# One 2 MB group of output weights loaded with a pattern whose outermost dimension counts 8

## The chip, the core and the metric

The kernel runs on one NeuronCore of a Trainium2 chip. The core has a matrix engine (TensorE, in the profile PE for the products and PEld for loading the stationary operand), VectorE (DVE), ScalarE (ACT), GpSimd (POOL) and SyncE (SP), which here does nothing but issue transfers. Sixteen DMA engines carry the data from the chip's memory (HBM) into the on-chip memory, whose first axis is 128 partitions. The metric is the device time of one execution in microseconds (us).

## The reference

One decoding step of a block: a layer norm, grouped-query attention over a cached K and V, a gated feed-forward branch, and a residual. Everything is float32.

```python
xn = layernorm(x)                               # x: [2, 1, 512]
q = (xn @ wq)                                   # 32 heads of 128
k, v = repeat(k_cache, 4), repeat(v_cache, 4)   # caches: [2, 8 kv heads, 32768, 128]
p = softmax(q k^T * 128**-0.5)
s = (p v).reshape(2, 1, 4096) @ wo              # wo: [4096, 512]
h = relu(xn @ w1 + b1) ** 2                     # w1: [512, 1792]
g = silu(h @ w2 + b2)
return x + s * g
```

The two caches are 268 MB each (256 MiB); with the weights the kernel reads 561 MB and writes 4 KB.

## The kernel before

**Streaming.** There are 16 sequences s (8 kv heads x 2 batch rows; hkv, b = divmod(s, 2)). Each is cut into 4 chunks of 8,192 positions, so there are 64 chunks of K and 64 of V, 4 MB each. A chunk is one transfer: 128 partitions, 32 KB for each. K has two buffers (pool "k"), V has two (pool "v"). A list `loads` holds all transfers in a fixed order, and `issue` sends the next ones on SP's queue as long as the pool of the first has a free buffer; `give`, called after the last use of a buffer, frees one and calls `issue` again. So the order on SP is that of the list, and nothing overtakes.

**One chunk.** `scores` (K): VectorE transposes the chunk in 32 x 32 blocks (L258), TensorE multiplies it with the queries (L263). After the fourth chunk `softmax` runs on VectorE and ScalarE; `probs` transposes the probabilities on TensorE. `values` (V) multiplies them with the V chunk four steps later (L319). At the end of a sequence `values` divides by the sum and puts the sequence's four head outputs into columns of `oT` (L331): partition = position in the head, column = head.

**The output projection.** The 4,096 rows of wo are handled in four groups of 1,024 rows (8 heads), `wo0` to `wo3`, 2 MB each. In a group, partition p holds rows 8p to 8p + 7 of it, one piece of 16 KB: so 16 consecutive partitions hold one head. The head outputs must be brought to the same layout. After every second kv head (L332) VectorE forms `om`: for each of the group's 8 heads, the head's column times a 0/1 selector `sele` (which of 16 blocks of 8 positions a position lies in), 128 x 128 numbers (L335). TensorE multiplies it with `selj` (which of 8 places in the block, L338) and ScalarE copies the result into `oW` (L339). `project` then multiplies `oW[:, i, j]` with `wo` (L401), eight steps for each group.

**The end.** The list's last transfers are: V chunk 60, wo0, V chunk 61, wo1, V chunk 62, V chunk 63 in two halves, wo2, and wo3 in four transfers: rows 0 to 5 of each partition's eight (1.5 MB, L122), then rows 6 and 7 in three pieces of columns (L124: 256, 128 and 128 columns). The program ends with the projections of groups 0 to 2, the first part of group 3, and then for each of the three pieces: projection, product with the gate (L414), a small matmul that also adds the residual (L415), a copy (L416). The result goes out at L417.

The instructions of an engine run in the order in which they are written in the program.

## Time and profile before

| | |
|---|---|
| time, median of 3 runs | 1321.92 us (1321.65 to 1323.48) |
| the profiled execution | 1321.55 us, its span 1319.8 us |
| PE / PEld / DVE / ACT / POOL busy | 865.2 / 300.3 / 646.4 / 69.0 / 27.9 us |
| read from HBM | 561.00 MB, 425 GB/s over the span |
| transfers of wo | 3 of 2,048 KB, 1 of 1,536 KB, 1 of 256 KB, 2 of 128 KB |
| instruction transfers (queue q8) | 52 packets, 0.85 MB |

The span runs from the first to the last instruction in the trace; the profiled execution's own time also holds what lies around it. A page of the profile shows the busy time of each engine, the span in 40 slices (33 us each) with the mean busy share of the 16 DMA engines, the DMA queues, the chain of work that ended last, followed back from the end, and the costliest groups of instructions. A group's row reads: line, engine, operation, output <- input, shape and count | busy time, mean ns of one | idle time of the engine just before, and what ended it. The view of stages gives the same busy times and the DMA share for chosen stretches of the span. An instruction's line in the timeline shows its start, its length and, in brackets, the idle time before it with what ended that.

### The profile page before, as it was taken

Reading aid. Unit: us, or ns where it says so; the run is one execution under the profiler, and the core shown is the slowest. Engines: PE = TensorE matmul, PEld = TensorE weight load, DVE = VectorE, ACT = ScalarE, POOL = GpSimd, SP = SyncE. Lnnn points to the kernel's source line nnn. Section 1 sums busy time; section 2 is a strip of 40 time slices with the busy share of each in tenths; the row PEclk is TensorE's granted clock in tenths of the full one; section 3 lists DMA queues with packets and bytes.
Section 4 is the critical chain, followed back from the end, with each engine's and each line's share of the span. In section 5 each row is a group of like instructions: output and inputs, shape, how many; then the busy total and the mean of one; then the engine's idle time right before and its main releaser. Section 6 shows DMA issues by size and latency. Waiting matters only on the chain.

```text
span 1319.8 us, 15186 instructions
## 1 busy us (share of the span) xinstructions
PE 865.2 (66%) x6710; PEld 300.3 (23%) x6710; DVE 646.4 (49%) x699; ACT 69.0 (5%) x109; POOL 27.9 (2%) x141
## 2 busy tenths in 40 slices
PE   4677765765676666675676666576577657667575
PEld 1222221322222122221222122132222212122121
DVE  3765553554555365355445445455445536535510
ACT  0010000101001010000101000010100101010010
POOL 1000000000000000000000000000000000000000
PEclk9988777787877877877877987787888788788778
DMA  9999999999999999999999999999999999999996
GB/s 412 429 429 428 432 432 433 430 429 432 431 431 428 432 433 429 432 432 429 431 430 433 432 431 429 432 428 434 431 429 432 431 431 431 430 429 434 431 404 284
DMA packets 20626, 561.96 MB, mean 426 GB/s; under 512 B 2249, under 2 KB 3021, under 8 KB 3026
## 3 DMA queue, kind: packets, MB, share of 16 engines
q1 hardware_dynamic: 20548, 561.00, 99.0%
q8 instruction: 52, 0.85, 0.3%
q14 instruction: 12, 0.10, 0.0%
q10 hardware_dynamic: 14, 0.01, 0.0%
HBM read 561.00 MB, written 0.00 MB: 425 GB/s over the span
## 4 chain that ended last, share of the span: by engine, by line
DMA 73%; DVE 21%; PE 3%; issue 3%; DVEq 0%; SPq 0%; ACT 0%; ACTq 0%
DMA k<-in_A_k_cache 69%; DVE kt L258 20%; DMA wo<-in_A_wo 2%; DMA v<-in_A_v_cache 1%; PE q_ps L219 1%; PE o_ps L319 1%; DMA xt<-in_A_x 1%; DVEq L258 0%; PE sc L263 0%; PE y_ps L365 0%; PE qT_ps L230 0%; PE a_ps L401 0%; DVE qr L226 0%; PE s_ps L415 0%; PE y_ps L370 0%
## 5 line engine op out<-in xcount | busy, mean ns | idle before, releaser
L258 DVE STREAM_TRANSPOSE kt<-k 128x1024 f32<-128x1024 f32 x512 | 584.4, 1208 | 423.9 <-DMA k<-in_A_k_cache 422.4
L263 PE MATMUL sc<-kt,qz 128*32 128x256 f32 x4096 | 544.5, 459 | 351.5 <-DVE kt L258 338.7
L263 PEld LDWEIGHTS sc<-kt,qz 128*32 128x32 f32 x4096 | 179.7, 127 | 729.7 <-DVE kt L258 602.9
L319 PE MATMUL o_ps<-v,pT 128*16 128x512 f32 x2048 | 261.2, 605 | 13.3 <-DMA v<-in_A_v_cache 13.3
L319 PEld LDWEIGHTS o_ps<-v,pT 128*16 128x16 f32 x2048 | 69.6, 98 | 155.9 <-issue 125.6
L326 ACT COPY o_sb<-o_ps 128x512 f32<-128x512 f32 x16 | 9.4, 585 | 1080.9 <-PE o_ps L319 1080.9
L295 PE MATMUL pT_ps<-ident,p 128*128 128x128 f32 x128 | 30.2, 412 | 46.7 <-ACT p L282 46.7
L331 DVE COPY oT<-oT_ps 128x4 f32<-128x4 f32 x16 | 2.6, 163 | 99.0 <-PE oT_ps L330 99.0
L242 POOL COPY qz<-qT 32x16 f32<-32x16 f32 x128 | 25.1, 200 | 1060.1 <-PE sc L263 1038.8
L270 DVE TENSOR_REDUCE rm<-sc 128x1 f32<-128x1024 f32 x16 | 19.6, 1224 | 32.1 <-PE sc L263 32.1
L295 PEld LDWEIGHTS pT_ps<-ident,p 128*128 128x128 f32 x128 | 23.7, 213 | 50.8 <-ACT p L282 49.7
L282 ACT ACTIVATE p<-sc,nm 128x1024 f32<-128x1024 f32 x16 | 32.9, 2057 | 25.1 <-DVE nm L279 25.0
L330 PE MATMUL oT_ps<-rs,o_sb 128*128 128x4 f32 x128 | 16.9, 255 | 12.0 <-ACT o_sb L326 12.0
L330 PEld LDWEIGHTS oT_ps<-rs,o_sb 128*128 128x128 f32 x128 | 15.5, 191 | 26.7 <-ACT o_sb L326 26.7
L296 ACT COPY pT<-pT_ps 128x512 f32<-128x512 f32 x32 | 18.7, 585 | 25.0 <-PE pT_ps L295 25.0
L286 DVE TENSOR_SCALAR lh<-selh,l 128x4 f32<-128x4 f32 x16 | 3.7, 229 | 32.9 <-ACT p L282 32.8
L302 DVE RECIPROCAL r<-l_ps 128x4 f32<-128x4 f32 x16 | 2.9, 182 | 33.0 <-PE l_ps L300 33.0
L207 PE MATMUL xnT_ps<-ident,xn 128*128 128x128 f32 x4 | 1.1, 428 | 15.6 <-DVE xn L203 15.6
L226 DVE COPY qr<-q_ps 128x512 f32<-128x512 f32 x8 | 5.3, 690 | 10.3 <-PE q_ps L219 9.8
L219 PE MATMUL q_ps<-wq,xnT 128*32 128x512 f32 x64 | 9.7, 774 | 0.8 <-DVE xnT L208 0.8
L401 PE MATMUL a_ps<-wo,oW 128*32 128x512 f32 (+2 forms) x72 | 9.0, 548 | 1.4 <-DMA wo<-in_A_wo 1.4
L300 PE MATMUL l_ps<-lh,ones 128*128 128x4 f32 x32 | 9.1, 355 | 0.0
(72 smaller groups left out, 98.2 us busy)
## 6 DMA issues: line engine op xcount, KB each, us to landing
k<-in_A_k_cache SPq DMA_DIRECT2D x64, 4096.0 KB, 29.6
v<-in_A_v_cache SPq DMA_DIRECT2D x63, 4096.0 KB, 33.9
wq<-in_A_wq SPq DMA_DIRECT2D x2, 4096.0 KB, 16.7
w<-in_B_w SPq DMA_DIRECT2D x2, 3584.0 KB, 27.7
wo<-in_A_wo SPq DMA_DIRECT2D x3, 2048.0 KB, 26.2
v<-in_A_v_cache SPq DMA_DIRECT2D x2, 2048.0 KB, 18.7
wo<-in_A_wo SPq DMA_DIRECT2D x1, 1536.0 KB
wo<-in_A_wo SPq DMA_DIRECT2D x1, 256.0 KB, 26.6
```

The source lines that it names most:

```text
L219: nc.tensor.matmul(q_ps[32 * g:32 * g + 32, f, :], xnT[:, d, 0:32], wqt[:, d2, cc * 512:(cc + 1) * 512], start=(d == 0), stop=(d == ND - 1))
L242: nc.gpsimd.tensor_copy(t[:, c, :, lo:lo + REP], qT[32 * a:32 * a + 32, b, hkv].rearrange("p h e -> p e h"))
L258: nc.vector.transpose(r.rearrange("p e o w -> p o e w"), kt[:, lo:lo + NO, :].rearrange("p o (e w) -> p o e w", e=4))
L263: nc.tensor.matmul(sc[s][32 * g:32 * g + 32, t // 2, c0:c0 + 256], qz[s % 2][:, c, e, :], kts[g][:, e].rearrange("p o w -> p (o w)"), star ...
L270: nc.vector.tensor_reduce(rm, sc[s], axis=AX.XY, op=ALU.max)
L282: nc.scalar.activation(p.rearrange("p o w t -> p o t w"), sc.pop(s).rearrange("p b (t o w) -> p o (b t) w", t=2, w=32), AF.Exp, bias=nm, s ...
L295: nc.tensor.transpose(t_ps[:, j * P:(j + 1) * P], p[:, 4 * i + j].rearrange("p w t -> p (w t)"), ident)
L296: nc.scalar.copy(sb[:, :, 4 * i:4 * i + 4, :].rearrange("p r o h -> p o r h"), t_ps.rearrange("p (o r h) -> p o r h", o=4, h=REP))
L300: nc.tensor.matmul(t_ps[:, :REP], ones, lh, start=True, stop=True)
L319: nc.tensor.matmul(o[32 * g:32 * g + 16, :], pT[s][:, r0, 4 * i:4 * i + 4, :].rearrange("p o h -> p (o h)"), vt[:, lo:lo + 4, :].rearrange ...
L326: nc.scalar.copy(o_sb, o)
L330: nc.tensor.matmul(t_ps[:, :REP], o_sb[:, i * DH:(i + 1) * DH], r4[:, i, :], start=(i == 0), stop=(i == 3))
```

## The change

Group 2 (`WHALF`) is loaded with another pattern; all other groups stay as they were. Its 1,024 rows are written as (n y j): 16 blocks n of 64 rows, in each 8 blocks y of 8 rows j. The source is walked with y outermost (count 8, 16 KB apart), then n (count 16, 128 KB apart), then 16 KB in one piece; the destination is walked as before, partition by partition. So partition 16 y + n now holds rows 64 n + 8 y to 64 n + 8 y + 7 of the group. Head h of the group (rows 128 h to 128 h + 127) has n = 2 h and 2 h + 1, that is partitions 16 y + 2 h + z with z = 0, 1.

`om` for group 2 (kv head 5, sequences 10 and 11) is therefore written in the order (y, h, z) in place of (h, e). The tile of `om` is now declared as 128 x 128 for all groups and viewed in either order; the other six executions do the same as before. The matmul with `selj`, the copy to `oW` and `project` are unchanged.

```diff
+WHALF = 2
...
     def load_wo(i):
...
         src = wo[i * WG * P:(i + 1) * WG * P, :].rearrange("(p j) e -> p j e", p=P)
-        if i < NWG - 1:
+        if i == WHALF:
+            nc.sync.dma_start(t.rearrange("p j e -> p (j e)"),
+                              wo[i * WG * P:(i + 1) * WG * P, :].rearrange("(n y j) e -> y n (j e)", y=8, j=WG))
+        elif i < NWG - 1:
             nc.sync.dma_start(t, src)
...
-                m = work.tile([P, WG, P // WG], F32, tag="om", name=f"om{s}")
-                nc.vector.tensor_mul(m, oT[:, i * WG:(i + 1) * WG, b:b + 1].to_broadcast([P, WG, P // WG]),
-                                     sele[:, None, :].to_broadcast([P, WG, P // WG]))
+                m = work.tile([P, P], F32, tag="om", name=f"om{s}")
+                oh = oT[:, i * WG:(i + 1) * WG, b]
+                if i == WHALF:
+                    nc.vector.tensor_mul(m.rearrange("p (y h z) -> p y h z", y=8, z=2),
+                                         oh[:, None, :, None].to_broadcast([P, 8, WG, 2]),
+                                         sele.rearrange("p (z y) -> p y z", y=8)[:, :, None, :].to_broadcast([P, 8, WG, 2]))
+                else:
+                    nc.vector.tensor_mul(m.rearrange("p (h e) -> p h e", h=WG),
+                                         oh[:, :, None].to_broadcast([P, WG, P // WG]),
+                                         sele[:, None, :].to_broadcast([P, WG, P // WG]))
                 t_ps = misc(f"oW_ps{s}")
-                nc.tensor.matmul(t_ps[:, :WG], m.rearrange("p h e -> p (h e)"), selj, start=True, stop=True)
+                nc.tensor.matmul(t_ps[:, :WG], m, selj, start=True, stop=True)
                 nc.scalar.copy(oW[:, i, :, b], t_ps[:, :WG])
```

## The prediction

> **What bounds the kernel now.** I read the page first: the busy line, the slices, the DMA queues, the chain.

> ```profile
> span 1319.8 us, 15186 instructions
> PE 865.2 (66%) x6710; PEld 300.3 (23%) x6710; DVE 646.4 (49%) x699; ACT 69.0 (5%) x109; POOL 27.9 (2%) x141
> ...
> DMA  9999999999999999999999999999999999999996
> GB/s 412 429 429 428 432 432 433 430 429 432 431 431 428 432 433 429 432 432 429 431 430 433 432 431 429 432 428 434 431 429 432 431 431 431 430 429 434 431 404 284
> ...
> q1 hardware_dynamic: 20548, 561.00, 99.0%
> q8 instruction: 52, 0.85, 0.3%
> ...
> DMA 73%; DVE 21%; PE 3%; issue 3%; DVEq 0%; SPq 0%; ACT 0%; ACTq 0%
> ```

> No compute engine is near full; the 16 DMA engines are, in every slice but the last. 430 GB/s over 16 engines is 26.9 GB/s for one. At that pace 16,384 bytes, one partition's row of an output-weight group, take 0.609 us; a 2 MB group spread over 16 engines (eight rows each) takes 4.87 us, and the first part of the last group (1.5 MB, six rows of eight) 3.65 us. The kernel streams 561 MB, so only the amount and its spread over the engines count. The last slice, 284 GB/s, is where they don't all work to the end. Next: the stages of the tail (columns: start and end, length, busy time of PE, PEld, DVE, ACT, POOL, clock, mean DMA share, GB/s).

> ```profile
> 1300.00:1306.00 6.00, 3.75 (x36) 0.64 (x28) 0.00 (x0) 0.49 (x1) 0.00 (x0) 1.00 0.98 413
> 1306.00:1307.00 1.00, 0.85 (x8) 0.85 (x8) 0.00 (x0) 0.10 (x1) 0.00 (x0) 1.00 0.95 347
> 1307.00:1308.00 1.00, 0.33 (x4) 0.27 (x4) 0.46 (x2) 0.00 (x0) 0.00 (x0) 1.00 0.57 239
> ...
> 1310.00:1311.00 1.00, 0.91 (x6) 0.00 (x0) 0.00 (x0) 0.00 (x0) 0.00 (x0) 1.00 0.51 187
> 1311.00:1312.00 1.00, 0.00 (x0) 0.00 (x0) 0.00 (x0) 0.00 (x0) 0.00 (x0) 1.00 0.26 96
> 1312.00:1313.00 1.00, 0.74 (x8) 0.44 (x12) 0.00 (x0) 0.00 (x0) 0.00 (x0) 1.00 0.27 82
> 1313.00:1314.00 1.00, 1.00 (x12) 0.15 (x4) 0.00 (x0) 0.00 (x0) 0.00 (x0) 1.00 0.01 4
> ```

> The share falls in steps: eight engines are done at about 1306.9, four at 1311.0, four at 1313.1. So one half runs ahead of the other by 4.1 to 6.2 us. Where the lag may come from is in the queue rows above: 0.85 MB of instruction transfers, if they fall on eight engines only, are 106 KB each, 3.9 us at 26.9 GB/s. Last, the chain and the timeline of the end.

> ```profile
> 1285.71 26.42 DMA wo<-in_A_wo
> 1312.12 0.14 issue
> 1312.26 1.96 PE a_ps L401 x12
> ...
> 1317.37 0.28 DVE fin L416
> ```

> ```profile
> 1303.48 1.91 PE L319 MATMUL o_ps<-v,pT 128*16 128x512 f32 x16 [1.63 <-DMA v<-in_A_v_cache]
> ...
> 1308.28 0.17 ACT L339 COPY oW<-oW_ps 128x8 f32<-128x8 f32 x1 [2.18 <-PE oW_ps L338]
> ...
> 1308.84 2.07 PE L401 MATMUL a_ps<-wo,oW 128*32 128x512 f32 x13
> ...
> 1312.26 1.91 PE L401 MATMUL a_ps<-wo,oW 128*32 128x512 f32 x16 [1.35 <-DMA wo<-in_A_wo]
> ```

> Two things set the end. The last piece of v (1303.48) leads through its products and group 2's projection to 1308.84 + 2.07 = 1310.91, where PE is free. The first part of group 3 lands at 1312.12, and PE starts it 1.35 us late. From there to the span's end are 1319.8 - 1312.12 = 7.7 us, which nothing here changes; the last three pieces of group 3 land under that work.

> **The change part by part.** Group 2 (the loop's i == 2) is the last full transfer before group 3. Its source becomes 8 blocks x 16 rows x 16 KB. What is moved stays 128 rows, 2 MB, at the same place of SP's queue and with the same wait; the first part and the three pieces of group 3 stay behind it. SP issues as many instructions as before.

> ```profile
> L120 SPq DMA_DIRECT2D wo<-in_A_wo x3: 383/433/1076, 1240.7 to 1285.2; - x3
> ...
> L335 DVE TENSOR_TENSOR om<-oT,sele x8: 291/292/293, 321.6 to 1307.4; 128x128 f32<-128x128 f32 x8
> ...
> L226 DVE COPY qr<-q_ps 128x512 f32<-128x512 f32 x8 | 5.3, 690 | 10.3 <-PE q_ps L219 9.8
> ...
> L258 DVE STREAM_TRANSPOSE kt<-k 128x1024 f32<-128x1024 f32 x512 | 584.4, 1208 | 423.9 <-DMA k<-in_A_k_cache 422.4
> ```

> - Issue on SP: 0.4 to 1.1 us for such a transfer now. The new form might cost from 0.4 less to 1.1 us more. Behind it on SP are only group 3's four issues, and the piece of v ahead of it lands 18 us later (1303.48); taken as 0. Without that cover, 1.1 us.
> - The product with the selector (om): two of its eight executions get another order of reading. The copy with a repeated operand moves 512 elements in 0.69 us, so 128 in 0.17; twice the present 0.29 is the other end. Both executions belong to kv head 5 (sequences 10 and 11 of 16), long before the end, where VectorE waits 422 us in all for K. Taken as 0; uncovered, from -0.2 to +0.6 us. The matmul and copy behind it keep their shapes.
> - The spread over the engines. An outermost count of 8 lets the work be dealt out eightfold: eight engines carry 16 rows of group 2, 16 x 0.609 = 9.74 us, and eight carry none.

> [...] No run here shows a large transfer with such a count.

> Which half is that? No view names engines. [...]

> Now the sum. The half ahead ends at 1306.9, less 4.87 for group 3, 4.87 for group 2 and about 0.2 for small pieces: it begins group 2 at 1297.0. The price that no row shows is that of two engines writing into the same part of the on-chip memory. Now each engine has its own eight rows in every 128-row transfer; with 16 consecutive rows for each of eight engines that ends. The bounds: no sharing, each keeps 26.9 GB/s; or sharing in pairs, each gets half. The nearest rows are the windows: 413 GB/s at a share of 0.98 and 239 at 0.57 are both 26.2 to 26.3 GB/s for one busy engine, so the pace belongs to each path and not to the memory that is read. They don't say at which end of the path the limit sits. I take sharing in pairs: a path that never shows more than 27 GB/s is more easily halved than doubled.

> [...]

> Shared in pairs, group 2 takes 2 x 9.74 = 19.5 us, to 1316.5; the first part of group 3 ends 3.65 later, at 1320.15, 8.0 us after 1312.12. Half of group 2's rows are those that the other eight engines serve, and they are still at work there. While a third engine takes turns, the pairs' four rows each (8 x 0.609 = 4.87 us) take 7.3, to 1304.3: +2.4. On the next four rows the engines met have 1311.0 - 4.87 - 1304.3 = 1.8 or 1313.1 - 4.87 - 1304.3 = 3.9 us of work left, which adds 1.8 to 2.4. After that they are done. So 8.0 + 2.4 + 1.9 = 12.3 us later. PE waits for it, and the 7.7 us behind it stay. The profiled execution took 1321.55 (its span of 1319.8 and 1.75 around it), 0.4 under the median of 1321.92: **1321.55 + 12.3 = 1333.9 us.**

> **The rivals.**

> - No sharing (the other side: not slower). The half ahead ends at 1306.9 + 4.87 = 1311.8, the other at 1313.1 - 4.87 = 1308.2. The first part of group 3 now lands 1.0 before the last end (1313.1 - 1312.1), so at 1310.8; PE is free at 1310.91. PE starts at about 1311.05 in place of 1312.26: 1.2 us won, 1320.7 with the median as base. More than 1.35 can't be had, since the chain through the last v stands behind it: a gain of over 0.2% (2.6 us, about what a measurement can tell from no change) is all but excluded. For it: the imbalance is plain in the windows, and nothing in the trace shows two engines hindering each other. It decides as soon as sharing costs the eight less than 1.3 us of their 9.74.
> - Sharing only with the other half. If each of the eight first writes rows of its own paths and then those of the other eight, it reaches them at 1297.0 + 4.87 = 1301.9, and halves its pace while they work: 4.87 become 9.74, to 1311.6, first part of group 3 at 1315.3: 3.2 us later, 1325. It needs an order of rows that consecutive rows don't give.
> - The eight are those behind. They end at 1313.1 + 4.87: 1326.8 without sharing. [...]
> - The pattern is dealt to 16 engines after all, and nothing changes: 1321.9. For it: still 128 rows of 16 KB on the memory's side.

> **How the numbers follow.** Sharing in pairs 0.45 (its own range 1329.5, which is 1321.55 + 8.0 alone, to 1335.5, with 2.4 twice and 1.1 on SP); no sharing 0.32; sharing with the other half only 0.10; the wrong half 0.07; no effect 0.06. Slower by over 0.2% is 0.45 + 0.10 + 0.07 = 0.62; within it, the two others less 0.02 for a reading that chance puts lower: 0.36; faster 0.02. The range takes in both ends of the unknown price: from 1320.4, a little under the no-sharing case, to 1335.5.

> **What will show it.** In the windows of the tail, a share of about 0.5 from the time the other half is done, at 13 GB/s for a busy engine if paths are shared (share high, GB/s low), at 26 if not. The first part of group 3 lands at about 1324 (forecast) or 1310.8. PE's idle time ahead of group 2's and group 3's projections, now 1.35 us, grows to over 10. With sharing the last pieces of v land later too, by 3 to 5 us after 1303.48; without it they stay. The om rows stay near 0.3 us. The prediction is wrong if the packets of group 2 keep about 0.61 us each.

## The result and the profile after

The changed kernel takes 1336.51 us (median, 1336.40 to 1336.73) against 1321.83 us before on the same chip: a ratio of 1.0107, 95% interval 1.0095 to 1.0119, or 14.7 us more. The direction was forecast, the size was not: 1333.9 was said, with 1335.5 as the upper end. The profiled execution has a span of 1334.6 us (before 1319.8).

The stages of the tail after the change (columns as before: stretch, length, PE, PEld, DVE, ACT, POOL, clock, DMA share, GB/s; a packet counts in the stretch in which it begins, so a share can come out a little over 1):

```profile
1290.00:1296.00 6.00, 2.35 (x12) 0.48 (x16) 0.00 (x0) 0.00 (x0) 0.00 (x0) 0.50 0.99 423
1296.00:1300.00 4.00, 4.00 (x24) 0.67 (x16) 0.00 (x0) 0.00 (x0) 0.00 (x0) 0.57 1.12 279
1300.00:1304.00 4.00, 1.94 (x20) 0.37 (x16) 0.00 (x0) 0.00 (x0) 0.00 (x0) 1.00 0.99 213
1304.00:1308.00 4.00, 0.00 (x0) 0.00 (x0) 0.00 (x0) 0.00 (x0) 0.00 (x0) 0.78 0.95 197
1308.00:1312.00 4.00, 2.25 (x12) 0.49 (x16) 0.00 (x0) 0.00 (x0) 0.00 (x0) 0.50 0.91 199
1312.00:1316.00 4.00, 2.56 (x18) 1.22 (x10) 0.46 (x2) 0.58 (x1) 0.00 (x0) 0.87 0.81 167
1316.00:1320.00 4.00, 1.56 (x4) 0.13 (x3) 0.00 (x0) 0.17 (x1) 0.00 (x0) 0.56 0.54 170
1320.00:1324.00 4.00, 0.66 (x4) 0.20 (x8) 0.00 (x0) 0.00 (x0) 0.00 (x0) 0.50 0.32 116
1324.00:1328.00 4.00, 3.78 (x25) 0.84 (x21) 0.00 (x0) 0.00 (x0) 0.00 (x0) 0.66 0.15 55
```

The kernel before, over the first two of these stretches together:

```profile
1290.00:1300.00 10.00, 6.31 (x36) 1.32 (x40) 0.00 (x0) 0.00 (x0) 0.00 (x0) 0.53 1.02 436
```

Up to 1296 the rate is that of the kernel before. Then the share stays near 1 while the rate falls to half: 213 GB/s at 0.99 is 213 / (16 x 0.99) = 13.4 GB/s for a busy engine, where the kernel before had 26. All 16 engines are busy, and all are slow, not only the eight that carry group 2: in the trace's records of single packets, every 16 KB row that begins between 1297 and 1300 takes 1.16 to 1.27 us, and every 12 KB row (group 3) 0.94 to 0.96, where 0.61 and 0.46 are the rule in the kernel before. After 1316 the share falls in a long tail: few engines are left, and 116 / (16 x 0.32) = 22.7 GB/s says that most of their time they are no longer halved.

The last waits of PE (timeline) and the last chain:

```profile
1309.75 3.54 PE L324 MATMUL o_ps<-v,pT 128*16 128x512 f32 x16 [7.81 <-DMA v<-in_A_v_cache]
...
1323.34 3.58 PE L413 MATMUL a_ps<-wo,oW 128*32 128x512 f32 x16 [5.78 <-DMA wo<-in_A_wo]
...
1327.13 1.91 PE L413 MATMUL a_ps<-wo,oW 128*32 128x512 f32 x16 [0.22 <-DMA wo<-in_A_wo]
```

```profile
1285.06 0.77 SPq L122
...
1285.87 41.12 DMA wo<-in_A_wo
1327.00 0.14 issue
```

The last piece of v is used at 1309.75 in place of 1303.48, group 2 at 1323.34, and the first part of group 3 lands at 1327.00 in place of 1312.12: 14.9 us later. From there to the end are 7.6 us, as before (7.7). What was costed at nothing stayed so: SP's issue took 0.77 us (median of such a transfer before: 0.43) and the reordered product with the selector (L342) as long as the others:

```profile
L346 DVE TENSOR_TENSOR om<-oT,sele x6: 291/292/293, 321.4 to 1315.3; 128x128 f32<-128x128 f32 x6
L342 DVE TENSOR_TENSOR om<-oT,sele x2: 292/293/294, 947.6 to 1025.7; 128x128 f32<-128x128 f32 x2
```

### The profile page after: what moved, and what is told of

The parts are those of the page before. It is cut to its first block, busy times and chain, and to the rows that moved or that the text cites. A ratio compares the mean times of both kernels' runs of the same rounds, so it can differ in the third digit from the quotient of the medians.

```text
span 1334.6 us, 15186 instructions
## 1 busy us (share of the span) xinstructions
PE 867.2 (65%) x6710; PEld 300.4 (23%) x6710; DVE 646.2 (48%) x699; ACT 69.1 (5%) x109; POOL 27.9 (2%) x141
## 3 DMA queue, kind: packets, MB, share of 16 engines
q1 hardware_dynamic: 20540, 561.00, 98.7%
HBM read 561.00 MB, written 0.00 MB: 420 GB/s over the span
## 4 chain that ended last, share of the span: by engine, by line
DMA 73%; DVE 21%; PE 3%; issue 2%; DVEq 0%; SPq 0%; ACTq 0%; ACT 0%
DMA k<-in_A_k_cache 68%; DVE kt L263 20%; DMA wo<-in_A_wo 3%; DMA v<-in_A_v_cache 1%; PE q_ps L224 1%; PE o_ps L324 1%; DMA xt<-in_A_x 1%; DVEq L263 0%; PE sc L268 0%; PE y_ps L377 0%; PE qT_ps L235 0%; PE a_ps L413 0%; DVE qr L231 0%; PE s_ps L427 0%; PE y_ps L382 0%
## 5 line engine op out<-in xcount | busy, mean ns | idle before, releaser
L335 PE MATMUL oT_ps<-rs,o_sb 128*128 128x4 f32 x128 | 16.9, 255 | 12.0 <-ACT o_sb L331 12.0
L335 PEld LDWEIGHTS oT_ps<-rs,o_sb 128*128 128x128 f32 x128 | 15.5, 191 | 27.5 <-ACT o_sb L331 27.5
L231 DVE COPY qr<-q_ps 128x512 f32<-128x512 f32 x8 | 5.3, 690 | 10.3 <-PE q_ps L224 9.8
## 6 DMA issues: line engine op xcount, KB each, us to landing
wo<-in_A_wo SPq DMA_DIRECT2D x3, 2048.0 KB, 26.3
```

The costliest lines, as they stand in the source:

```text
L335: nc.tensor.matmul(t_ps[:, :REP], o_sb[:, i * DH:(i + 1) * DH], r4[:, i, :], start=(i == 0), stop=(i == 3))
```

## The experiments

**The disputed price by itself.** A kernel with loads only, one after the other. Its load functions, without the rest of it:

```diff
+    def plain(n, col):
+        nc.sync.dma_start(t[:n], w[:8 * n, :].rearrange("(p j) e -> p (j e)", j=8))
...
+    def eight(n, col):
+        nc.sync.dma_start(t, w.rearrange("(n y j) e -> y n (j e)", y=8, j=8))
...
+    def near(n, col):
+        nc.sync.dma_start(t, wo[:1088, :].rearrange("(y n j) e -> y n (j e)", y=8, j=8)[:, :16])
...
+    def quarters(n, col):
+        v = w.rearrange("(m r y j) e -> m y r (j e)", m=4, r=4, j=8)
+        for m in range(4):
+            nc.sync.dma_start(t[32 * m:32 * m + 32], v[m])
...
+    def far16(n, col):
+        nc.sync.dma_start(t, w.rearrange("(b a j) e -> a b (j e)", b=8, j=8))
...
+    def split(n, k, col):
...
+        nc.sync.dma_start(t[:n], w[:8 * n, :].rearrange("(q y j) e -> y q (j e)", y=k, j=8))
...
```

`eight` is the changed kernel's pattern, `near` gives each engine 256 KB in one piece of HBM, `far16` has an outermost count of 16.

> This kernel leaves out the whole computation: it only loads parts of wo, one transfer after the other, each after the one before has landed, and writes x's memory out again. Order, each of the first five twice: the group's plain 2 MB load; the changed kernel's pattern (outermost 8, blocks 128 KB apart); outermost 8 with each block of 16 rows contiguous in HBM; the changed kernel's pattern cut into four transfers of 32 partitions (outermost 8, four partitions for each); 16 engines with blocks far apart (256 KB). Then smaller ones: 32 and 64 partitions with outermost 8, 64 with 4, 32 with 2, 8 with 2, 4 with 2. Theory T (engines that write into the same part of the on-chip memory share its path): plain and far apart about 430 GB/s while running, packets of 16 KB in 0.61 us; the pattern and its contiguous variant both about 110 GB/s, packets 1.22 us; four quarters about 215 GB/s, packets 0.61. Of the small ones, 32 with 8 and 32 with 2 run at 0.61, 64 with 8 at 1.22, 8 with 2 at 0.61, 4 with 2 at 1.22. Theory S (the order of reading in HBM): the pattern, the quarters and the far-apart load all slow, the contiguous variant at 0.61. Theory W (eight engines instead of 16, and some of them those that are behind, no sharing): every packet of 16 KB takes 0.61, the patterns with 8 about 215 GB/s.

Stretches from within the transfers (DVE, POOL, clock, DMA share, GB/s). In order: plain; the pattern; contiguous in HBM; quarters; outermost 16; 64 partitions dealt in eights to eight; 64 partitions to four; 32 to two; 8 to two; 4 to two:

```profile
14.50:19.50 5.00, 0.00 (x0) 0.00 (x0) 1.00 0.83 344
24.00:40.00 16.00, 0.00 (x0) 0.00 (x0) 1.00 0.51 111
68.00:84.00 16.00, 0.00 (x0) 0.00 (x0) 1.00 0.51 114
112.00:118.00 6.00, 0.00 (x0) 0.00 (x0) 1.00 0.51 218
136.00:144.00 8.00, 0.00 (x0) 0.00 (x0) 1.00 1.08 227
167.00:173.00 6.00, 0.00 (x0) 0.00 (x0) 1.00 0.47 109
179.00:194.00 15.00, 0.00 (x0) 0.00 (x0) 1.00 0.26 57
200.00:208.00 8.00, 0.00 (x0) 0.00 (x0) 1.00 0.12 53
212.50:214.50 2.00, 0.00 (x0) 0.00 (x0) 1.00 0.11 49
217.20:219.00 1.80, 0.00 (x0) 0.00 (x0) 1.00 0.07 18
```

A share of 0.51 is eight engines. The pattern gives them 111 / (16 x 0.51) = 13.6 GB/s each, and reading in one piece changes nothing (114). The same eight blocks in the same order of reading, but written in fours, run at 26.7 GB/s each (218 at 0.51). So S falls, and W cannot be all: the place of writing decides. Nor is an engine slow by itself when it writes 16 neighbouring partitions: 32 partitions dealt to two engines run at 53 / (16 x 0.12) = 27.6 GB/s each. With 4 partitions for two engines, the four packets took 0.94 to 1.39 us, near the 1.22 that T had said; over their stretch it is 18 / (16 x 0.07) = 16 GB/s for a busy engine. The others fall into two kinds. A busy engine moved 13.6 to 14.5 GB/s with the pattern (111 at 0.51) and with 64 partitions dealt in eights (109 at 0.47) or sixteens (57 at 0.26). It moved 26 to 28 where a transfer held 32 partitions or 8, with at least four for each engine (218 at 0.51, 53 at 0.12, 49 at 0.11). Which partitions share a path, no view shows.

Two things came out otherwise than expected. The load with an outermost count of 16 was said to run at 430 under T; it ran at 227 GB/s with all engines busy. My estimate of the reason, from the half pace of 64 partitions dealt in eights (109 at 0.47): each engine gets eight neighbouring partitions here too and is met there by another; no view shows which engine writes where. Of the two forms here that use all 16 engines, only the plain one, with 128 rows in one dimension on both sides, ran at full pace (344 / (16 x 0.83) = 25.9 GB/s for a busy engine, against 227 / (16 x 1.08) = 13.1). And plain loads of 2 MB that stand alone show 344 over a stretch that holds their ends.

**The same in the kernel.** Group 2 in four transfers of 32 partitions:

```diff
-            nc.sync.dma_start(t.rearrange("p j e -> p (j e)"),
-                              wo[i * WG * P:(i + 1) * WG * P, :].rearrange("(n y j) e -> y n (j e)", y=8, j=WG))
+            parts = wo[i * WG * P:(i + 1) * WG * P, :].rearrange("(q r y j) e -> q y r (j e)", q=4, r=4, j=WG)
+            for q in range(4):
+                nc.sync.dma_start(t[32 * q:32 * q + 32].rearrange("p j e -> p (j e)"), parts[q])
```

(with the selector's product in the matching order, four small instructions for each of the two executions).

> Group 2 as in the changed kernel, the same eight blocks read in the same order by the same count of eight, but as four transfers of 32 partitions, so that each engine writes four neighbouring partitions in each. Theory T: no pairs meet any more; what is left is the meeting with the other eight engines and the doubled work of the eight: 1324 to 1329 us, packets of 0.61 us except where the two halves meet. Theory S: as slow as the changed kernel, 1335 to 1338, packets at 1.2 us. Theory W: as slow as eight engines with double work make it, 1326 to 1328 if two of the eight are behind, and the changed kernel's time is then left unexplained by 9 us.

Measured: 1331.36 us, ratio 1.0074 (1.0059 to 1.0089): 9.8 us lost in place of 14.7. That lies above the 1324 to 1329 of T. Its tail:

```profile
1296.00:1302.00 6.00, 5.44 (x40) 1.05 (x32) 0.00 (x0) 0.00 (x0) 0.00 (x0) 0.79 1.00 428
1302.00:1304.00 2.00, 0.19 (x4) 0.13 (x8) 0.00 (x0) 0.00 (x0) 0.00 (x0) 1.00 1.03 310
1304.00:1310.00 6.00, 4.57 (x28) 1.59 (x20) 0.46 (x2) 0.76 (x2) 0.00 (x0) 0.90 0.88 186
```

Full pace lasts to 1302, which is when the first of the eight (at group 2 since 1297.0) have written their eight rows on partitions 0 to 63 (8 x 0.609 = 4.87 us) and begin on 64 to 127. Then the engines are halved again: 186 / (16 x 0.88) = 13.2 GB/s for a busy one. Beside plain loads (below) the same dealing showed the same two sides: 422 GB/s on partitions 0 to 63, 203 on 64 to 127.

**The place.** `WHALF = 0` in place of 2: the pattern on group 0.

> The pattern on group 0, which is loaded about 45 us before the end with 16 MB still to follow, in place of group 2. If transfers bound the whole stream, the place doesn't matter: the engines lose the same time, 1333 to 1338 us. If only the tail is exposed and the queues ahead take the loss up elsewhere: 1322 to 1326.

Measured: 1344.3 us, ratio 1.0170 (1.0153 to 1.0187), 22.7 us lost; both expectations missed, the first of them in the right direction. Its stages, and its last chain:

```profile
1270.00:1290.00 20.00, 5.56 (x32) 1.03 (x32) 0.00 (x0) 0.00 (x0) 0.00 (x0) 0.67 1.00 224
...
1304.00:1311.00 7.00, 6.92 (x44) 1.34 (x36) 0.00 (x0) 0.00 (x0) 0.00 (x0) 0.68 0.41 150
```

```profile
1259.66 43.00 DMA v<-in_A_v_cache
...
1302.71 6.55 PE o_ps L324 x32
...
1309.28 0.33 SPq L101
...
1309.66 17.40 DMA v<-in_A_v_cache
```

The half pace is there as well, and a second loss comes behind it: from 1304 to 1311 the engines are 59% idle. A chunk of V lands 43.00 us after its issue, PE uses it until 1309.26, and only that frees the buffer for which the next load waits (issued at 1309.28). So here, earlier in the stream, the pattern costs more, not less.

**Who is held up.** Again loads only: a first load and, right behind it without a wait, two plain loads over all 16 engines into other buffers. The first loads:

```diff
...
+    def blocks(lo, n, k):
+        nc.sync.dma_start(t[lo:lo + n], w[:8 * n, :].rearrange("(q y j) e -> y q (j e)", y=k, j=8))
...
+    def low_pairs():
+        blocks(0, 64, 8)
+    def low_apart():
+        blocks(0, 32, 8)
+        blocks(32, 32, 8)
+    def high_apart():
+        blocks(64, 32, 8)
+        blocks(96, 32, 8)
+    def full_pattern():
+        blocks(0, 128, 8)
...
```

> This kernel leaves out the whole computation and only loads. Ten groups of transfers, each group after the one before has landed: a first load into one buffer, and right behind it two plain 1.5 MB loads over all 16 engines (12 KB rows, alone 0.46 us each) into other buffers. The first load is, twice each: plain 2 MB over 16 engines; 64 partitions (0 to 63) dealt to eight engines in eights, so that they meet in pairs; the same 64 partitions dealt in fours, so that they don't meet; partitions 64 to 127 dealt in fours, where each of the eight meets one of the other eight; the changed kernel's full pattern. The question is why all 16 engines ran at half pace in the changed kernel. Theory L (sharing slows only the engines that write into the same part): beside the pairs on 0 to 63 the other eight engines stay at 0.46 us for a 12 KB row, and the core moves about 109 + 217 = 326 GB/s while both run. Theory B (a full path holds up the others too): they slow down as well, to 0.9 us, and the core moves about 220 GB/s. In both: the load dealt in fours on 0 to 63 leaves everybody at full pace (430 GB/s while 16 run), on 64 to 127 every engine is halved (about 217).

Stretches in which the first load and the plain ones run together: plain; in eights on 0 to 63 (both times); in fours on 0 to 63; in fours on 64 to 127; the full pattern:

```profile
22.00:28.00 6.00, 0.15 (x1) 0.00 (x0) 1.00 0.99 423
35.00:40.00 5.00, 0.00 (x0) 0.00 (x0) 1.00 0.99 211
52.00:57.00 5.00, 0.00 (x0) 0.00 (x0) 1.00 1.07 229
80.00:84.00 4.00, 0.00 (x0) 0.00 (x0) 1.00 1.00 422
92.00:97.00 5.00, 0.00 (x0) 0.00 (x0) 1.00 0.99 203
127.00:131.00 4.00, 0.00 (x0) 0.00 (x0) 1.00 1.00 143
```

In fours on 0 to 63 disturbs nobody (422; 377 at a share of 0.94 the other time, 25 GB/s for a busy engine); in fours on 64 to 127 the core falls to 203 (215 the other time). From these two I take it that the other eight engines write to 64 to 127 and are met there only. Yet the load in eights on 0 to 63 brings the whole core to 211 to 229 GB/s. Theory L wanted 326. The trace's records of single packets say the same: between 35 and 40 us no 12 KB row of the plain loads took less than 0.75 us (median 0.95), where 0.46 is the rule from 22 to 28. So the load in eights on 0 to 63 held up all 16 engines: theory B. Where on the way they are held up, no view shows. With the full pattern it is a third, 143 (149 the other time).

**Which eight.** The kernel before, with half of group 2 left out (partitions 64 to 127 are filled with zeros, so the result of that group is not the reference's), the other half dealt in fours to the eight engines of the pattern:

```diff
-        if i < NWG - 1:
+        if i == 2:
+            half = wo[i * WG * P:i * WG * P + 512, :].rearrange("(q r y j) e -> q y r (j e)", q=2, r=4, j=WG)
+            for q in range(2):
+                nc.sync.dma_start(t[32 * q:32 * q + 32].rearrange("p j e -> p (j e)"), half[q])
+            nc.gpsimd.memset(t[64:], 0.0)
+        elif i < NWG - 1:
```

> The kernel before, but of group 2 only 1 MB is loaded, into partitions 0 to 63, dealt in fours to the eight engines of the pattern; the other half of the group is left out (filled with zeros on GpSimd). So the eight have the same eight rows as before and nobody meets anybody; the other eight have 4.87 us less. If the eight of the pattern are those ahead, as the prediction took it: all transfers end by 1308.4, PE starts the last group at about 1311, 1320.3 us. If some of the eight are those behind: a few engines still work to 1311 or 1313, the share of DMA there is their number over 16, and the time stays at 1321 to 1322.

Measured: 1322.01 us, ratio 1.0006 (0.9997 to 1.0016): nothing won with 1 MB less. Its tail:

```profile
1307.00:1308.00 1.00, 0.39 (x3) 0.38 (x4) 0.43 (x2) 0.00 (x0) 0.00 (x0) 1.00 0.28 105
1309.00:1310.00 1.00, 1.00 (x12) 0.34 (x5) 0.00 (x0) 0.00 (x0) 0.00 (x0) 1.00 0.18 69
1310.00:1311.00 1.00, 0.64 (x5) 0.00 (x0) 0.00 (x0) 0.00 (x0) 0.00 (x0) 1.00 0.12 49
1311.00:1312.00 1.00, 0.21 (x4) 0.19 (x8) 0.00 (x0) 0.00 (x0) 0.00 (x0) 1.00 0.12 40
```

Engines that have nothing of group 2 must be done by about 1308.2 (1313.1 - 4.87). A share of 0.12 from 1310 to 1312 is two engines: two of the eight belong to those that are behind. The 0.18 before it (1309 to 1310) is a third: by the trace's records of single packets its rows of group 2 begin at 1299.95 and those of the last two at about 1302.6, while the other five begin at about 1296.5.

**Sharing without eight engines.** An outermost count of 16, so that all 16 engines carry eight rows as before:

```diff
-                              wo[i * WG * P:(i + 1) * WG * P, :].rearrange("(n y j) e -> y n (j e)", y=8, j=WG))
+                              wo[i * WG * P:(i + 1) * WG * P, :].rearrange("(n y j) e -> y n (j e)", y=16, j=WG))
```

(again with the selector's product in the matching order).

> The changed kernel with an outermost count of 16 in place of 8 (partition 8 y + n holds rows 128 n + 8 y to 128 n + 8 y + 7). All 16 engines carry eight rows of group 2 as in the kernel before, but each writes eight neighbouring partitions, and two engines meet all the way. If the cost were that of eight engines with double work: no loss, 1321 to 1323 us. If it is sharing that holds up everybody: half pace (about 215 GB/s at a full share) from 1297, when the first reach group 2, until the last have left it. The first half of the engines leaves it at 1306.8; those behind then still have about 1.0 us of v, and their eight rows take 9.74 in place of 4.87: to 1317.5; the first part of group 3 lands 3.65 later at 1321.2, about 9 us after 1312.1: 1329 to 1332 us.

Measured: 1331.45 us, ratio 1.0067 (1.0050 to 1.0084), inside what sharing foretold.

```profile
1298.00:1306.00 8.00, 3.37 (x32) 0.67 (x24) 0.00 (x0) 0.00 (x0) 0.00 (x0) 0.93 1.05 219
...
1316.00:1320.00 4.00, 2.18 (x9) 0.40 (x12) 0.00 (x0) 0.00 (x0) 0.00 (x0) 0.50 0.69 199
```

Half pace (219 / (16 x 1.05) = 13.0 GB/s for a busy engine) with eight rows for each of 16 engines. A part of its loss, and of the quarters', is PE's: groups 2 and 3 are multiplied in one run from 1318.38, 5.62 us for 32 instructions at a granted clock of 0.50 up to 1320, where the kernel before had the clock at 1.00 and took 1.91 for 16. The quarters' run is the same: 5.97 us from 1317.93.

```profile
1318.38 5.62 PE L413 MATMUL a_ps<-wo,oW 128*32 128x512 f32 x32 [1.82 <-DMA wo<-in_A_wo]
```

No version that beats the kernel before came out of this. A pure gain is bounded by the 1.35 us that PE waits for group 3 there, and the eight engines that carried group 2 include two that are behind (the share of 0.12 from 1310 to 1312).

## Why the prediction was wrong in size

- **The bound, and what was costed at nothing**: right. DMA bounds the tail, the last 7.6 us are unchanged, issue and selector cost nothing that shows.
- **Eight engines**: right; a share of 0.51 for the pattern alone.
- **Sharing in pairs halves the eight**: right in the pace, and it was the open price: 111 GB/s for the pattern by itself, 13.4 to 13.6 GB/s for an engine, half of 26.9. That they meet two by two was the prediction's estimate; no view shows which engines meet.
- **The eight of the pattern as the half ahead**, with which the sum begins (group 2 from 1297.0): no run shows it. With half the group left out, the share of 0.12 to 1312 says that two of the eight are behind, and a third is some 3 us behind the rest. The two reach group 2 last and then have 16 rows each. The rival of the wrong half was priced without sharing only.
- **The meeting with the other half, +2.4 and +1.9**: not what the runs showed. The load in eights on 0 to 63 beside plain loads held up all 16 engines (211 to 229 GB/s against 423), and in the changed kernel every 16 KB row that begins between 1297 and 1300 took 1.16 to 1.27 us. So the last piece of v, which I had forecast 3 to 5 us late, came 6.3 us late. Rows at a third of the pace, from which the 2.4 was worked out, did not occur in the changed kernel: no 16 KB row that began after 1290 took over 1.27 us, where a third would be 1.83. Beside two plain loads the full pattern did bring all to a third (143 GB/s); why it didn't here was not tried.
- **The signs**: the idle time of PE ahead of group 2's and group 3's projections was to grow to over 10 us; it came to 5.78 + 0.22 = 6.0, since the last v had come late as well. The share of about 0.5 at 13 GB/s for a busy engine didn't come either: the share was near 1 while the pace was halved, and when it had come down to 0.54 (1316 to 1320) a busy engine moved 170 / (16 x 0.54) = 19.7 GB/s.

So the step that failed is what the forecast added to the eight's own 19.5 us: the meeting with the other half, on the footing that all eight were ahead. It had group 2 complete at 1316.5 + 2.4 + 1.9 = 1320.8. Its last row ended at 1322.8, because two engines had started late under a half pace that held for all. That the forecast came within 2.6 us of the time is luck in part: 4.3 us for a meeting that did not happen that way stand where late engines cost 6.3.

With these two put right the sum closes. At half pace a row of 16 KB takes 16,384 / 13.4 GB/s = 1.22 us. From 1297.0 the engines behind have 1303.5 - 1297.0 = 6.5 us of v left, which take 13: to 1310.0 (measured 1309.75). The six ahead leave group 2 after 16 x 1.22 = 19.5 us, at 1316.5. By then the two have written (1316.5 - 1309.75) / 1.22 = 5.5 rows; the other 10.5 run at full pace, 10.5 x 0.609 = 6.4: group 2 is complete at 1322.9 (PE starts it at 1323.34), and the first part of group 3, 3.65 later, at 1326.6. It landed at 1327.00. This sum is made after the result. Its parts were measured in separate kernels: the pace, the holding up, the two engines. It is coarse in the middle: by the trace's records five engines left group 2 at 1315.0 to 1315.4, the third late one at 1320.8, the last two at 1322.5 and 1322.8.

The rivals without sharing and without effect fell with the first experiment (13.6 GB/s, and eight engines in place of 16). The rival of the wrong half was a quarter true, and it matters only together with the sharing. The rival with its meeting in the other half alone gave 1325; the kernel that does it (quarters) took 1331.4, since there too all 16 were halved, two engines began late, and PE multiplied groups 2 and 3 at half the clock.

## What to carry to other kernels

Before dealing a transfer out by its outermost dimension, load it by itself and with plain loads behind it. Here the dealing halved the pace of the engines that did it (13.6 GB/s for the pattern, 14.5 for 64 partitions in eights), and the second also slowed the rows of the plain loads behind it (0.95 us for 12 KB in place of 0.46). A rebalancing of engines needs to be known engine by engine: a mean share of 0.57 shows how many are behind, not which. And price the gain's ceiling first: here a wait of 1.35 us was all that could be won, against 14.7 lost.

## What the runs showed that was not expected

- A load in eights on 64 partitions took the whole core from 423 to 211 to 229 GB/s, the full pattern beside plain loads to 143, with all engines counted busy. A DMA share of 0.99 or 1.00 stood beside all three rates, 423, 211 and 143: it takes the rate to tell them apart.
- The same 2 MB over all 16 engines ran at 344 GB/s in its plain form and at 227 with a source whose outermost dimension is 16. For a busy engine that is 25.9 and 13.1 GB/s: the count of engines did not settle the rate.
- The same pattern 2 MB for 2 MB cost 14.7 us at the end of the stream and 22.7 us some transfers earlier, where a buffer that came free late left the engines 59% idle for 7 us. Why the half pace itself lasted longer there was not tried.
